# A fused attention and two-layer kernel: the second layer's weights are converted in the first layer's middle blocks and kept in DRAM

## The chip, the cores and the metric

The program runs on one core of one Trainium2 chip. The metric is the device time of one execution in microseconds (us), the median of the runs.

## What is computed

A recurrent linear attention over 4 batches, 8 heads, 768 steps and head size 48, then two feed-forward layers on the 3072 tokens (384 wide, 2048 hidden). The first has an ELU, the second h * cos(h). The weights of both layers arrive as float64.

```python
for t in range(S):
    cur = np.einsum('bhd,bhe->bhde', u[None] * kt, vt)
    y[:, :, t] = np.einsum('bhd,bhde->bhe', rt, state + cur)
    state = w[None, :, :, None] * state + np.einsum('bhd,bhe->bhde', kt, vt)
...
h = x @ w_in
g = np.where(h > 0.0, h, alpha * (np.exp(np.minimum(h, 0.0)) - 1.0))
x = (g @ w_out).astype(np.float32)
...
h = x @ w_in
g = h * np.cos(h)
return (g @ w_out).astype(np.float32)
```

## The kernel before

**Tiling.** Tokens go in 6 chunks of 512 (128 steps of 4 batches). A layer's 2048 hidden columns go in 16 tiles of 128 (`NF = 16`). The main loop runs over t from 0 to 193; one pass is called a slot here. `layer, block, f = t // 96, t // 16, t % 16`: a block is one layer on one chunk, 16 slots. Blocks 0 to 5 (slots 0 to 95) are the first layer, blocks 6 to 11 (slots 96 to 191) the second. In slot t TensorE does the 9 matmuls of 512 columns of `ffn_in` for tile f (line 300), the nonlinearity follows on ScalarE and VectorE, `split_g` cuts its result g into a rounded high part gh (ScalarE, line 307) and the rest gl (line 308), and two slots later TensorE does the 9 (first layer) or 12 (second) matmuls of `ffn_out_t` or `ffn_out` (lines 355, 364). Every product is made of three matmuls of high and low parts.

**Attention.** The attention of chunks 1 to 5 is laid into the slots of blocks 0 to 4, from chunk 2 on one unit (a batch pair and a head pair) for every two slots: an even slot has the Gram matmuls (line 194) and the masked copy of their result by VectorE (`copy_predicated`, line 199), an odd one the matmuls with values and state (lines 213, 217, 244) with the copy yu on ScalarE (line 227) and the state update st on VectorE (line 236). GpSimd prepares later units (lines 156, 157, 164, 181). A unit is loaded six slots ahead of its Gram matmuls and prepared four slots ahead. Block 5 has no attention. At a block's last slot `split_x` cuts the next chunk's x into xh (ScalarE, line 288, 3 operations) and xl (VectorE, line 289, 3 operations); the next block's first matmuls need them.

**Weights.** A weight tile (768 columns of float64 on 128 partitions, 768 KB) is loaded into wraw (`load_w`) and goes through seven operations of 768 elements: Abs (ScalarE, line 83), two `tensor_scalar` (VectorE, lines 89 and 92, `conv_low`), two `scalar_tensor_tensor` (VectorE, lines 99 and 102, `conv_high`), the rounded high part (ScalarE, line 111) and the low part by subtraction (GpSimd, line 112). The parts lie in wh and wl, and TensorE reads them. The first layer's 16 tiles are converted ahead of block 0 and in it. The second layer's are converted from block 5 on, into the same buffers, each behind the first layer's last use of it: in block 5 about one tile per slot (`convert(steps2)`), the last ones in block 6 at one step per slot. In blocks 0 and 5 gl is made by GpSimd (`busy`), elsewhere by VectorE.

**Order.** The whole order is written by hand: each engine runs its instructions in the order in which the program issues them, and waits at the first whose inputs or buffers are not there. All DMAs are issued by SyncE (SP), in one order.

Of the kernel before, what the change touches and what calls it, by code (L numbers as in the profile page):

```python
# [20 lines left out]
P = 128  # L21
# [18 lines left out]
def fused_kernel(ctx: ExitStack, tc: tile.TileContext, rk, nat, wcol, urow, r, k, v, wu, w1, w2, out):  # L40
# [9 lines left out]
    x2d = [dram.tile([P, KC, TB], F32, name=f"x2d{c}") for c in range(NC)]  # L50

    # ---------------------------------------------------------------- tables
# [24 lines left out]
    # A weight comes as a float64: words (low, high). Its magnitude's high word, read as a float32,  # L77
    # is monotone, so clamping that clamps the weight to float32's range.
# [18 lines left out]
    def conv_high(layer, f):  # L97
        t, x = wc_st[layer, f]
        nc.vector.scalar_tensor_tensor(  # L99
            out=x, in0=t[:, :, 1], scalar=-(1 << 30), in1=x, op0=ALU.bitwise_and, op1=ALU.bitwise_or  # L100
        )
        nc.vector.scalar_tensor_tensor(  # L102
            out=x, in0=t[:, :, 0], scalar=29, in1=x, op0=ALU.logical_shift_right, op1=ALU.bitwise_or
        )

    def conv_split(layer, f, eng):
        x = wc_st.pop((layer, f))[1]
        x = x.bitcast(F32)
        hi = wpool.tile([P, 2 * DM], F32R, tag=f"wh{f}", name=f"wh{f}")
        lo = wpool.tile([P, 2 * DM], F32R, tag=f"wl{f}", name=f"wl{f}")  # L110
        nc.scalar.activation(out=hi, in_=x, func=AF.Copy)  # L111
        eng.tensor_tensor(out=lo, in0=x, in1=hi.bitcast(F32), op=ALU.subtract)  # L112
        wt[layer, f] = (hi, lo)

    def conv_steps(layer):
        """Steps that turn a layer's weights into their two parts, three tiles at a time in turn."""

        def high(f):
            conv_high(layer, f)
            if f + 3 < NF:  # L120
                w_loads.append((layer, f + 3))

        steps = []
        for n in range(NF + 2):
            for f, step, fn in (
                (n - 2, "split", lambda f: conv_split(layer, f, nc.gpsimd)),
                (n - 1, "low", lambda f: conv_low(layer, f)),
                (n - 1, "high", high),
                (n, "abs", lambda f: conv_abs(layer, f)),
            ):  # L130
                if 0 <= f < NF:
                    steps.append((step, lambda fn=fn, f=f: fn(f)))
        return steps

    # ------------------------------------------------------------- attention
# [4 lines left out]
    def a_load(c, hb, j):  # L140
        if c == 0:
            # the first chunk lies where the last weight tiles will
            n = NF - 2 * HP + hb * HP + ORDER.index(j)
            trk = wpool.tile([RP, 2, 2, C], F32, tag=f"wl{n}", name="trk")
            tnat = wpool.tile([P, 3, 2, 2, D], F32, tag=f"wh{n}", name="tnat")
# [116 lines left out]
    def a_pack(c, hb, j):  # L262
        """Rows of a finished pair of heads into x: 96 of a k-tile, or the last 32 of each."""
# [9 lines left out]
        else:  # L273
            # the first chunk's last pair goes by itself: the first layer waits for it
# [9 lines left out]
    # ---------------------------------------------------------- feed-forward  # L284
# [40 lines left out]
    # cos(h) = sin(h + pi/2), the turn nearest to it taken off in two parts  # L325
# [43 lines left out]
    # ---------------------------------------------------------- general path  # L369
    def general():  # L370
        """Any decay: the recurrence step by step, then both layers in float32."""
# [40 lines left out]
        for layer in range(2):  # L412
            for f in range(NF):
# [4 lines left out]
                w = wpool.tile([P, 2 * DM], F32, tag=f"w{'hl'[layer]}{f}", name="wf")  # L418
# [61 lines left out]
    def tables():  # L480
        """pw[:, :, i] = w ** (i - 64), w128 = w ** 128, wn[s, h, d] = w ** (64 + s)"""
# [29 lines left out]
    def count_safe():  # L511
        """safe = 1 where every decay's powers over a chunk lie in range"""
# [14 lines left out]
    with tc.manual_schedule():  # L527
# [33 lines left out]
        steps, steps2 = conv_steps(0), conv_steps(1)  # L561
        put_off = []

        def convert(queue, n=None, hold=False):
            """The next n steps or those up to a tile's first, which is put off to the end of the slot."""
# [17 lines left out]
        # the first chunk's attention, its stages a unit apart  # L583
# [56 lines left out]
        for t in range(NT + 2):  # L640
            layer, block, f = t // L, t // NF, t % NF
            busy = layer == 0 and block in (0, NC - 1)
            if t < NT:
                ph = ffn_in(layer, f, xs[block], "G" if layer and f % 2 else "h")
            if layer == 0 or t == L:
# [4 lines left out]
                if t == 2 * NF:  # L650
                    count_safe()
                elif block == NC - 1:
                    if f == 0:
                        load_w(1, 0)
                        load_w(1, 1)
                        load_w(1, 2)
                    if f > 0:
                        convert(steps2)
# [16 lines left out]
            if layer == 0:  # L675
                end_slot()
            n = block + 1
# [12 lines left out]
            turning = t > L + 1  # L690
# [6 lines left out]
            (ffn_out if layer else ffn_out_t)(layer, f, *gs.pop(t - 2), acc)  # L697
            if f == NF - 1 and layer == 0:
# [11 lines left out]
            if turning:  # L710
                convert(steps2, 1)
                end_slot()
# [63 lines left out]
```

## Time and profile before

| | before |
|---|---|
| median of 3 runs | 1006.22 us (1004.83 to 1008.23) |
| span of the profiled execution | 1009.6 us |
| TensorE matmuls, busy | 946.1 us (94%) |
| VectorE busy | 700.6 us (69%) |
| ScalarE busy | 462.5 us (46%) |
| GpSimd busy | 272.5 us (27%) |
| moved by DMA | 70.35 MB |

The profile is of one execution, a run of its own; its span is the time from its first to its last instruction and lies 3.4 us above the median of the runs. Busy is the time in which an engine had an instruction under way. Matmuls overlap in the records, so a busy TensorE does not say how fast it runs; the time between the starts of two slots does.

### The profile page before, as it was taken

To read this page: it belongs to the slowest core of one execution; us is meant where nothing else is said; L and a number is where in the kernel's file an instruction comes from. 1 tells how busy PE (TensorE), PEld (TensorE's weight loads), DVE (VectorE), ACT (ScalarE), POOL (GpSimd) and SP (SyncE) were. 2 spreads that over 40 slices of the span, in tenths; PEclk is the share of its full clock that TensorE was granted. 3 is DMA by queue.
4 is the path that set the end of the run, shared out by engine and by line. 5 is a ranking of instruction groups with operands and counts; after the bars stand their busy time and mean duration, and the time that the engine had idled before them with its cause. 6 is when DMAs were issued, how large, how long until landed. Compare 5 with 4: busy or idle time off the path is not lost.

```text
span 1009.6 us, 13386 instructions
## 1 busy us (share of the span) xinstructions
PE 946.1 (94%) x5018; PEld 780.5 (77%) x5018; DVE 700.6 (69%) x1096; ACT 462.5 (46%) x770; POOL 272.5 (27%) x258
## 2 busy tenths in 40 slices
PE   6498889999999999999997779999999999999997
PEld 5366657777777777777775558899999999999996
DVE  6799974445544544534379999977877777777775
ACT  2454535334433433443465565544444445444443
POOL 6898973322322322211046541000000000000000
PEclk7599889999999999999999899999999999999999
DMA  9654620302322131130234321010010010100001
GB/s 251 197 166 148 195 74 28 108 23 73 89 68 75 54 91 44 42 91 3 106 108 165 114 84 63 1 63 1 1 63 1 1 63 1 63 1 1 32 1 35
DMA packets 28793, 70.35 MB, mean 70 GB/s; under 512 B 3760, under 2 KB 11568, under 8 KB 28720
## 3 DMA queue, kind: packets, MB, share of 16 engines
q1 hardware_dynamic: 28720, 69.42, 21.6%
q8 instruction: 41, 0.67, 0.3%
q14 instruction: 32, 0.26, 0.1%
HBM read 55.25 MB, written 9.44 MB: 64 GB/s over the span
## 4 chain that ended last, share of the span: by engine, by line
PE 72%; DVE 16%; issue 5%; POOL 2%; DMA 2%; ACT 2%; SPq 0%; DVEq 0%; ACTq 0%; POOLq 0%
PE ph L300 32%; PE acc L364 18%; PE acc L355 15%; DVE wx L99 4%; PE ys L217 3%; PE G L194 2%; PE ys L213 2%; DVE wx L92 2%; DVE g L320 1%; DVE wx L89 1%; DMA xraw<-yu 1%; DVE xl L289 1%; DVE wx L102 1%; DVE gl L308 1%; DVE trk L170 1%
## 5 line engine op out<-in xcount | busy, mean ns | idle before, releaser
L300 PE MATMUL ph<-xh,wh 128*128 128x512 f32 x576 | 229.5, 398 | 17.7 <-DVE g L320 17.7
L300 PE MATMUL ph<-xl,wh 128*128 128x512 f32 x576 | 228.8, 397 | 2.1 <-DVE xl L289 2.0
L300 PE MATMUL ph<-xh,wl 128*128 128x512 f32 x576 | 226.8, 394 | 0.0
L307 ACT ACTIVATE gh<-g 128x512 fp32r<-128x512 f32 x192 | 120.6, 628 | 191.6 <-DVE g L320 130.8
L308 DVE TENSOR_TENSOR gl<-g,gh 128x512 fp32r<-128x512 f32 x161 | 116.5, 724 | 68.6 <-ACT gh L307 68.5
L300 PEld LDWEIGHTS ph<-xh,wh 128*128 128x128 f32 x576 | 108.8, 189 | 42.9 <-DVE g L320 20.1
L364 PE MATMUL acc<-wh,gl 128*128 128x384 f32 x384 | 129.1, 336 | 3.7 <-DVE gl L308 3.7
L300 PEld LDWEIGHTS ph<-xl,wh 128*128 128x128 f32 x576 | 109.2, 190 | 28.4 <-DVE xl L289 3.5
L364 PE MATMUL acc<-wl,gh 128*128 128x384 f32 x384 | 129.4, 337 | 0.0
L364 PE MATMUL acc<-wh,gh 128*128 128x384 f32 x384 | 129.0, 336 | 0.0
L345 ACT ACTIVATE r<-r,halfpi 128x512 f32<-128x512 f32 x96 | 69.7, 726 | 125.0 <-DVE r L339 125.0
L300 PEld LDWEIGHTS ph<-xh,wl 128*128 128x128 f32 x576 | 109.1, 189 | 19.9
L355 PE MATMUL acc<-gh,wh 128*128 128x512 f32 x288 | 123.9, 430 | 0.4 <-ACT gh L307 0.4
L355 PE MATMUL acc<-gl,wh 128*128 128x512 f32 x288 | 114.8, 399 | 0.3 <-DVE gl L308 0.2
L355 PE MATMUL acc<-gh,wl 128*128 128x512 f32 x288 | 114.4, 397 | 0.0
L181 POOL TENSOR_SCALAR_AFFINE_SELECT A<-a 128x512 f32<-128x512 f32 x48 | 47.2, 983 | 241.4 <-DVE a L177 239.2
L333 DVE SCALAR_TENSOR_TENSOR r<-kk,ph 128x512 f32<-128x512 int32 x96 | 65.8, 686 | 56.3 <-ACT kk L328 56.2
L313 ACT ACTIVATE n<-ph 128x512 f32<-128x512 f32 x96 | 56.9, 593 | 94.9 <-PE ph L300 94.8
L328 ACT ACTIVATE kk<-ph 128x512 int32<-128x512 f32 x96 | 57.7, 601 | 73.9 <-PE ph L300 73.8
L112 POOL TENSOR_TENSOR wl<-wx,wh 128x768 fp32r<-128x768 f32 x32 | 74.1, 2317 | 45.6 <-ACT wh L111 30.4
L320 DVE SCALAR_TENSOR_TENSOR g<-e,ph 128x512 f32<-128x512 f32 x96 | 65.4, 681 | 27.8 <-ACT e L315 27.4
L347 DVE TENSOR_TENSOR g<-r,ph 128x512 f32<-128x512 f32 x96 | 65.8, 685 | 19.2 <-ACT r L345 19.2
(73 smaller groups left out, 1373.6 us busy)
## 6 DMA issues: line engine op xcount, KB each, us to landing
wraw<-in_w SPq DMA_DIRECT2D x32, 768.0 KB, 4.4
tnat<-in_nat SPq DMA_DIRECT2D x48, 288.0 KB, 4.4
trk<-in_rk SPq DMA_DIRECT2D x48, 224.0 KB, 4.3
x2d<-osb SPq DMA_DIRECT2D x6, 768.0 KB, 4.2
xraw<-x2d SPq DMA_DIRECT2D x6, 768.0 KB, 5.2
out_y<-yo SPq DMA_DIRECT2D x12, 384.0 KB, 3.1
xraw<-yu SPq DMA_DIRECT2D x22, 144.0 KB, 2.8
xraw<-yu SPq DMA_DIRECT2D x24, 32.0 KB, 1.9
```

Source lines behind the costliest of these rows:

```text
L112: eng.tensor_tensor(out=lo, in0=x, in1=hi.bitcast(F32), op=ALU.subtract)
L300: nc.tensor.matmul(ph, w[:, cs], z, start=(n == 0), stop=(n == 3 * KC - 1))
L307: nc.scalar.activation(out=gh, in_=g, func=AF.Copy)
L308: eng.tensor_tensor(out=gl, in0=g, in1=gh.bitcast(F32), op=ALU.subtract)
L313: nc.scalar.activation(out=n, in_=ph, func=AF.Relu, scale=-1.0)
L320: nc.vector.scalar_tensor_tensor(out=g, in0=e, scalar=-1.0, in1=ph, op0=ALU.add, op1=ALU.max)
L328: nc.scalar.activation(out=kk, in_=ph, func=AF.Copy, scale=1.0 / TWO_PI, bias=0.25)
L333: nc.vector.scalar_tensor_tensor(out=r, in0=kk, scalar=-C1, in1=ph, op0=ALU.mult, op1=ALU.add)
L345: nc.scalar.activation(out=r, in_=r, func=AF.Sin, bias=halfpi)
L347: nc.vector.tensor_tensor(out=g, in0=r, in1=ph, op=ALU.mult)
L355: nc.tensor.matmul(acc[m], w[:, cs], g, start=(f == 0 and n == 0), stop=(f == NF - 1 and n == 2))
L364: nc.tensor.matmul(acc[m][:, 0:DM], g[:, ts], w[:, DM:2 * DM], start=(f == 0 and n == 0), stop=(f == NF - 1 and n == 2),)
```

## The change

The second layer's 16 weight tiles are converted in slots 16 to 79, a tile in four slots. `second_weights` adds one part at the end of each slot: part 0 the two `tensor_scalar`, part 1 the first `scalar_tensor_tensor` (`conv_top`), part 2 the second (`conv_rest`), part 3 the high part on ScalarE, the low part on VectorE (it was on GpSimd) and the Abs of the next tile. Both parts are written over the raw tile, and the tile (768 KB) is stored to DRAM (`w2d`) in the part 0 that follows; the load of the tile after next waits for that store, since it takes the same buffer. In block 5 `fetch_weight(f)` reads tile f back into the first layer's buffer behind the last `ffn_out_t` that uses it, 14 slots ahead of its first use. wh and wl become halves of one tile. Nothing is converted in blocks 5 and 6 any more, and in block 5 gl is made by VectorE.

```diff
+    w2d = [dram.tile([P, 4 * DM], F32, name=f"w2d{f}") for f in range(NF)]
...
-        hi = wpool.tile([P, 2 * DM], F32R, tag=f"wh{f}", name=f"wh{f}")
-        lo = wpool.tile([P, 2 * DM], F32R, tag=f"wl{f}", name=f"wl{f}")
+    def split_w(x, parts, eng):
+        hi, lo = parts[:, 0:2 * DM], parts[:, 2 * DM:]
         nc.scalar.activation(out=hi, in_=x, func=AF.Copy)
         eng.tensor_tensor(out=lo, in0=x, in1=hi.bitcast(F32), op=ALU.subtract)
...
+    def second_weights(slot):
+        f, part = slot // 4, slot % 4
+        if slot == 0:
+            load_w(1, 0)
+            load_w(1, 1)
+            conv_abs(1, 0)
+        if part == 0:
+            if f > 0:
+                nc.sync.dma_start(out=w2d[f - 1], in_=split_tiles.pop(f - 1).bitcast(F32))
+            if f < NF:
+                conv_low(1, f)
+        elif part == 1:
+            if f + 2 < NF:
+                load_w(1, f + 2)
+            conv_top(1, f)
+        elif part == 2:
+            conv_rest(1, f)
+        else:
+            t, x = wc_st.pop((1, f))
+            parts = t.rearrange("p n l -> p (n l)").bitcast(F32R)
+            split_w(x.bitcast(F32), parts, nc.vector)
+            split_tiles[f] = parts
+            if f + 1 < NF:
+                conv_abs(1, f + 1)
+
+    def fetch_weight(f):
+        w = new_weight(f)
+        nc.sync.dma_start(out=w.bitcast(F32), in_=w2d[f])
+        wt[1, f] = (w[:, 0:2 * DM], w[:, 2 * DM:])
...
-            busy = layer == 0 and block in (0, NC - 1)
+            busy = layer == 0 and block == 0
...
-                elif block == NC - 1:
-                    if f == 0:
-                        load_w(1, 0)
-                        load_w(1, 1)
-                        load_w(1, 2)
-                    if f > 0:
-                        convert(steps2)
...
             if layer == 0:
                 end_slot()
+                if NF <= t <= 5 * NF:
+                    second_weights(t - NF)
...
             (ffn_out if layer else ffn_out_t)(layer, f, *gs.pop(t - 2), acc)
+            if layer == 0 and c == NC - 1:
+                fetch_weight(f)
...
-            if turning:
-                convert(steps2, 1)
-                end_slot()
```

VectorE at the end of block 1, from the last operations of slot 30 over slot 31 to the first of slot 32, before (g is the ELU, gl the rest of g, xl the rest of the next chunk's x):

```order
L170 TENSOR_TENSOR trk<-trk,pw 112x512
L320 SCALAR_TENSOR_TENSOR g<-e,ph 128x512
L308 TENSOR_TENSOR gl<-g,gh 128x512
L236 SCALAR_TENSOR_TENSOR st<-st,pows,ys 48x2x48 x2
L320 SCALAR_TENSOR_TENSOR g<-e,ph 128x512
L289 TENSOR_TENSOR xl<-xraw,xh 128x512 x3
L308 TENSOR_TENSOR gl<-g,gh 128x512
```

and now (wx is a weight tile under conversion, wraw the raw tile):

```order
L219 TENSOR_TENSOR trk<-trk,pw 112x512
L369 SCALAR_TENSOR_TENSOR g<-e,ph 128x512
L106 SCALAR_TENSOR_TENSOR wx<-wraw,wx 128x768
L357 TENSOR_TENSOR gl<-g,gh 128x512
L285 SCALAR_TENSOR_TENSOR st<-st,pows,ys 48x2x48 x2
L369 SCALAR_TENSOR_TENSOR g<-e,ph 128x512
L117 TENSOR_TENSOR wraw<-wx,wraw 128x768
L338 TENSOR_TENSOR xl<-xraw,xh 128x512 x3
L357 TENSOR_TENSOR gl<-g,gh 128x512
```

One operation of the conversion stands behind the ELU of each slot; in slot 31 the subtraction stands between the ELU and the three xl.

ScalarE over slot 31, the same place, before (n and e belong to the ELU):

```order
L313 ACTIVATE n<-ph 128x512
L315 ACTIVATE e<-n 128x512
L227 ACTIVATE yu<-ys 112x256
L288 ACTIVATE xh<-xraw 128x512 x3
L307 ACTIVATE gh<-g 128x512
```

and now:

```order
L362 ACTIVATE n<-ph 128x512
L364 ACTIVATE e<-n 128x512
L276 ACTIVATE yu<-ys 112x256
L116 ACTIVATE wraw<-wx 128x768
L84 ACTIVATE wx<-wraw 128x768
L337 ACTIVATE xh<-xraw 128x512 x3
L356 ACTIVATE gh<-g 128x512
```

The high part of one tile and the Abs of the next stand between yu and the three xh.

SP in block 1 from slot 22 to slot 26, before (trk and tnat are a unit's loads, xraw<-yu the packing of attention results into x):

```order
L269 DMA xraw<-yu 32x256
L270 DMA xraw<-yu 16x256
L271 DMA xraw<-yu 16x256
L272 DMA xraw<-yu 32x256
L149 DMA trk<-in_rk 112x512
L150 DMA tnat<-in_nat 128x576
L149 DMA trk<-in_rk 112x512
L150 DMA tnat<-in_nat 128x576
L149 DMA trk<-in_rk 112x512
L150 DMA tnat<-in_nat 128x576
```

and now:

```order
L318 DMA xraw<-yu 32x256
L319 DMA xraw<-yu 16x256
L320 DMA xraw<-yu 16x256
L321 DMA xraw<-yu 32x256
L198 DMA trk<-in_rk 112x512
L199 DMA tnat<-in_nat 128x576
L198 DMA trk<-in_rk 112x512
L199 DMA tnat<-in_nat 128x576
L160 DMA w2d_77<-wraw 128x1536
L75 DMA wraw<-in_w 128x1536
L198 DMA trk<-in_rk 112x512
L199 DMA tnat<-in_nat 128x576
```

The store of a tile and the load into its buffer stand between the loads of two units.

## Rows read from the trace of the kernel before

**Rows 1.** Busy time by stretch: blocks 2, 5, 6 and 7; clock, DMA last.

```profile
248.90:335.89 86.99, 86.79 (x516) 67.21 (x514) 42.51 (x88) 36.10 (x62) 24.13 (x32) 1.00 0.22 67
502.47:592.07 89.60, 74.13 (x289) 56.51 (x288) 82.65 (x75) 50.54 (x79) 50.41 (x27) 0.94 0.35 124
592.07:663.90 71.83, 68.31 (x331) 59.40 (x331) 64.60 (x93) 39.90 (x63) 9.97 (x5) 1.00 0.09 34
663.90:730.57 66.67, 66.67 (x338) 60.49 (x338) 51.86 (x86) 31.93 (x53) 0.00 (x0) 1.00 0.07 24
```

**Rows 2.** Timeline, TensorE in block 4 behind its attention: first matmuls of two slots.

```profile
490.11 0.39 PE L300 MATMUL ph<-xh,wh 128*128 128x512 f32 x1
...
494.23 0.39 PE L300 MATMUL ph<-xh,wh 128*128 128x512 f32 x1
```

**Rows 3.** Waits: us, times, longest; block 5, then block 6.

```profile
PE ph L300 <- DVE g L320: 13.0, 10, 1.8
...
PE acc L364 <- DVE gl L308: 2.9, 4, 1.1
```

**Rows 4.** Timeline, operations of the conversion at different places.

```profile
80.66 1.24 DVE L99 SCALAR_TENSOR_TENSOR wx<-wraw,wx 128x768 int32<-128x768 int32 x1
...
525.36 2.51 DVE L102 SCALAR_TENSOR_TENSOR wx<-wraw,wx 128x768 int32<-128x768 int32 x1
...
607.01 0.83 ACT L111 ACTIVATE wh<-wx 128x768 fp32r<-128x768 f32 x1
...
613.40 0.55 DVE L89 TENSOR_SCALAR wx<-wx 128x768 f32<-128x768 f32 x1
613.99 0.56 DVE L92 TENSOR_SCALAR wx<-wx 128x768 int32<-128x768 int32 x1
...
617.77 0.95 DVE L99 SCALAR_TENSOR_TENSOR wx<-wraw,wx 128x768 int32<-128x768 int32 x1
...
620.89 0.90 ACT L83 ACTIVATE wx<-wraw 128x768 f32<-128x768 f32 x1
```

**Rows 5.** Timeline of block 2, VectorE and ScalarE in slots 45 and 46.

```profile
320.17 0.82 DVE L308 TENSOR_TENSOR gl<-g,gh 128x512 fp32r<-128x512 f32 x1 [0.76 <-ACT gh L307]
...
323.42 0.64 DVE L236 SCALAR_TENSOR_TENSOR st<-st,pows,ys 48x96 f32<-48x96 f32 x2 [2.43 <-ACT yu L227]
...
324.08 0.69 DVE L320 SCALAR_TENSOR_TENSOR g<-e,ph 128x512 f32<-128x512 f32 x1
...
325.26 0.63 ACT L307 ACTIVATE gh<-g 128x512 fp32r<-128x512 f32 x1 [1.88 <-PE acc L355]
...
325.93 0.69 DVE L308 TENSOR_TENSOR gl<-g,gh 128x512 fp32r<-128x512 f32 x1 [1.16 <-ACT gh L307]
...
328.04 0.78 DVE L199 COPY_PREDICATED A<-mask,G 128x256 f32<-128x256 uint32 x2 [1.41 <-PE G L194]
```

**Rows 6.** Timeline, end of slot 31 and slot 32.

```profile
247.12 1.66 ACT L288 ACTIVATE xh<-xraw 128x512 fp32r<-128x512 f32 x3
...
248.52 1.89 DVE L289 TENSOR_TENSOR xl<-xraw,xh 128x512 fp32r<-128x512 f32 x3
...
248.90 0.39 PE L300 MATMUL ph<-xh,wh 128*128 128x512 f32 x1
...
249.37 0.39 PE L300 MATMUL ph<-xl,wh 128*128 128x512 f32 x1
...
251.34 0.19 PE L518 MATMUL okp<-ok,ones 112*1 112x4 f32 x2 [0.20 <-DVE ok L514]
```

**Rows 7.** Page, DMA issues: KB each, median us to landing.

```profile
x2d<-osb SPq DMA_DIRECT2D x6, 768.0 KB, 4.2
xraw<-x2d SPq DMA_DIRECT2D x6, 768.0 KB, 5.2
```

**Rows 8.** Timeline, a unit's load on SP, and its first use on GpSimd.

```profile
315.15 0.40 SPq L149 DMA_DIRECT2D trk<-in_rk  x1
...
341.52 0.60 POOL L156 TENSOR_TENSOR tnat<-tnat 128x192 f32<-128x192 f32 x1
```

More of the change, by code (lines that the diff above doesn't have):

```diff
@@ L95, in conv_low, with conv_top @@
         )
-    def conv_high(layer, f):
+    def conv_top(layer, f):
         t, x = wc_st[layer, f]
@@ L101, in conv_high, with conv_rest @@
         )
+    def conv_rest(layer, f):
+        t, x = wc_st[layer, f]
         nc.vector.scalar_tensor_tensor(
@@ L104, in conv_high, with new_weight, conv_split @@
         )
-    def conv_split(layer, f, eng):
-        x = wc_st.pop((layer, f))[1]
-        x = x.bitcast(F32)
-        hi = wpool.tile([P, 2 * DM], F32R, tag=f"wh{f}", name=f"wh{f}")
-        lo = wpool.tile([P, 2 * DM], F32R, tag=f"wl{f}", name=f"wl{f}")
+    def conv_high(layer, f):
+        conv_top(layer, f)
+        conv_rest(layer, f)
+    def split_w(x, parts, eng):
+        hi, lo = parts[:, 0:2 * DM], parts[:, 2 * DM:]
         nc.scalar.activation(out=hi, in_=x, func=AF.Copy)
         eng.tensor_tensor(out=lo, in0=x, in1=hi.bitcast(F32), op=ALU.subtract)
-        wt[layer, f] = (hi, lo)
+    def new_weight(f):
+        return wpool.tile([P, 4 * DM], F32R, tag=f"w{f}", name=f"w{f}")
+    def conv_split(layer, f):
+        x = wc_st.pop((layer, f))[1]
+        w = new_weight(f)
+        split_w(x.bitcast(F32), w, nc.gpsimd)
+        wt[layer, f] = (w[:, 0:2 * DM], w[:, 2 * DM:])
     def conv_steps(layer):
@@ L125, in conv_steps @@
             for f, step, fn in (
-                (n - 2, "split", lambda f: conv_split(layer, f, nc.gpsimd)),
+                (n - 2, "split", lambda f: conv_split(layer, f)),
                 (n - 1, "low", lambda f: conv_low(layer, f)),
@@ L133, in conv_steps @@
         return steps
+    split_tiles = {}
+    def second_weights(slot):
[23 more added lines that the diff above has]
+    def fetch_weight(f):
+        w = new_weight(f)
+        nc.sync.dma_start(out=w.bitcast(F32), in_=w2d[f])
+        wt[1, f] = (w[:, 0:2 * DM], w[:, 2 * DM:])
     units = {}
@@ L143, in a_load @@
             n = NF - 2 * HP + hb * HP + ORDER.index(j)
-            trk = wpool.tile([RP, 2, 2, C], F32, tag=f"wl{n}", name="trk")
-            tnat = wpool.tile([P, 3, 2, 2, D], F32, tag=f"wh{n}", name="tnat")
+            both = wpool.tile([P, 4 * DM], F32, tag=f"w{n}", name="both")
+            m = 4 * C
+            trk = both[0:RP, 0:m].rearrange("p (x b t) -> p x b t", x=2, b=2)
+            tnat = both[:, m:m + 12 * D].rearrange("p (x e b d) -> p x e b d", x=3, e=2, b=2)
         else:
@@ L411, in general @@
         ws = {}
-        for layer in range(2):
-            for f in range(NF):
+        for f in range(NF):
+            both = wpool.tile([P, 4 * DM], F32, tag=f"w{f}", name="wf")
+            for layer in range(2):
                 load_w(layer, f)
@@ L417, in general @@
                 conv_high(layer, f)
-                w = wpool.tile([P, 2 * DM], F32, tag=f"w{'hl'[layer]}{f}", name="wf")
+                w = both[:, layer * 2 * DM:(layer + 1) * 2 * DM]
                 nc.scalar.activation(out=w, in_=wc_st.pop((layer, f))[1].bitcast(F32), func=AF.Copy)
@@ L560, in fused_kernel @@
                 items.setdefault((c - 1) * NF + it, []).append(fn)
-        steps, steps2 = conv_steps(0), conv_steps(1)
+        steps = conv_steps(0)
         put_off = []
@@ L689, in fused_kernel @@
                 continue
-            turning = t > L + 1
             layer, c, f = (t - 2) // L, (t - 2) // NF % NC, (t - 2) % NF
```

## The prediction

> **What bounds the kernel now.** I read the busy time by stretch first, a block at a time [rows 1]. In blocks 2 and 7 TensorE's busy time is the whole stretch (66.67 of 66.67 us) and VectorE has room (42.51 of 86.99): these blocks go at TensorE's pace. Blocks 5 and 6 don't: TensorE is busy in 74.13 of 89.60 us and in 68.31 of 71.83. In block 5 VectorE is busy in 82.65 of the 89.60 us, so VectorE sets the pace there; its granted clock column also falls to 0.94, a mix of TensorE's two levels, while every other block in the group shows 1.00.
>
> The waits say what TensorE waits for [rows 3]. In block 5 it waits 13.0 us in 10 pieces of up to 1.8 us for the ELU result, which stands on VectorE behind a tile's conversion; in block 6 it waits 2.9 us for gl at the conversion's steps. The timeline shows what a first-layer slot costs when nothing but the feed-forward is left in it: the slots behind block 4's last attention follow each other at 490.11 and 494.23, that is 4.12 us [rows 2].
>
> One operation of the conversion has several prices [rows 4]. The same `scalar_tensor_tensor` takes 0.95 us in the second layer, 1.24 us in block 0 beside GpSimd's small products, and 2.51 us in block 5 beside GpSimd's subtraction of a whole tile. The two `tensor_scalar` take 0.55 and 0.56, the Abs 0.90, the high part 0.83.
>
> **What the change removes.** Block 5 loses every conversion, so its 16 slots can go at the 4.12 us of [rows 2]: those slots have already what block 5 gets, gl on VectorE and no attention. 16 x 4.12 = 65.9, against 89.60: 23.7 us gained. VectorE then has an ELU and a gl per slot, 0.69 + 0.69 [rows 5], a third of the slot. Block 6 becomes like block 7: 71.83 - 66.67 = 5.2 us gained [rows 1]. The layer's switch lies in block 6 too; nothing of it but the conversion is slow for a reason that I can see, so I take all of it.
>
> **What it adds in blocks 1 to 4.** VectorE gets per tile 0.55 + 0.56, two operations of 0.95 to 1.24, and the subtraction, which no row shows on VectorE; as an operation with two inputs of 768 elements I take 0.95, its like in [rows 4], with 2.51 as the upper end. That is 4.0 to 4.6 us per four slots, about 1.1 us a slot. I ask what stands behind each piece. In an odd slot it comes after the ELU, which starts at 324.08 and takes 0.69; the next instruction, gl, waited 1.16 us for gh, and the one after it, the masked copy, waited 1.41 us for the Gram matmuls [rows 5]. Together that is 2.57 us of cover for a piece of about 0.95. In an even slot gl waited 0.76 and the state update after it 2.43 us: 3.19 us for a piece of 1.1 to 1.24. Delaying gl itself costs nothing, since TensorE uses it a slot later. So the pieces are hidden, and hidden even at 2.51 us each, barely.
>
> On ScalarE the high part and the Abs (0.83 + 0.90 = 1.73) stand every fourth slot, an odd one, between yu and gh, and gh waited 1.88 us there for its buffer [rows 5]. Hidden, with 0.15 left. On VectorE the subtraction waits for the high part, which ends about when the ELU ends.
>
> On SP a tile's store waits for the subtraction, and the next load of a raw tile waits until that store has landed; what stands behind it is a later unit's trk and tnat. A store of this size lands in 4.2 us [rows 7]. In the trace such a load was issued at 315.15, and GpSimd first used it at 341.52 [rows 8]. With the store issued at about the same time, the load would go out some 4.2 us later and still be over 20 us early. Hidden. SP runs ahead of the slots in this way, so the first two raw tiles, whose buffers are free by then, land before their Abs in slot 16.
>
> In block 5 each read-back is issued 14 slots before its use. At the 5.2 us of the same size [rows 7], one behind the other, the last lands 16 x 5.2 = 83 us after the first was issued at the end of slot 82. Its use is in slot 111, 28 slots of 4.12 to 4.17 us (66.67 / 16), some 116 us, after that. Hidden.
>
> **The step that is not hidden** is the last slot of blocks 1 to 4, where the order puts the last part ahead of the next chunk's x. Before, the three xh start at 247.12 and the three xl at 248.52, and TensorE's first two kinds of matmul of block 2 start at 248.90 and 249.37, right behind them [rows 6]. Now ScalarE does 1.73 us first: the first xh (1.66 / 3 = 0.55) ends at 247.12 + 1.73 + 0.55 = 249.4, and TensorE starts 0.5 us late. VectorE puts the subtraction ahead: xl starts at 248.52 + 0.95 = 249.5, the first is ready at 250.1, 0.75 us late, the last at 251.4. In slot 32 a small matmul (okp) also waits for VectorE, which is now about 1.1 us late. I take 1.1 us for each of the four, since the others lack okp but the fourth lacks the attention matmuls that would cover a part: 4.4 us. The bounds are 0, if x is read early enough by another path, and 1.73 + 0.95 = 2.7 each, 10.7 in all, if both engines' additions add up.
>
> **Sum.** 1009.6 - 23.7 - 5.2 + 4.4 = 985.1 us for the span, a gain of 24.5. The profiled execution is 3.4 us above the median of the runs; I take the same gain off the median: 1006.2 - 24.5 = 981.7 us. From no change at the seams (-28.9) to the full seams (-18.2) that is 977.3 to 988.0.
>
> **Rivals.** (1) The pieces don't fit: VectorE and GpSimd hold each other up. For it: the same instruction took 0.95, 1.24 and 2.51 us according to what GpSimd did at the time [rows 4]. Against: in block 2 GpSimd has only small operations (24.13 us in 86.99). It decides when an odd slot's piece passes 2.57 us; at 2.51 with a gl drawn out from 0.69 to 0.82 [rows 5] a pair of slots would lose some 0.2 to 0.3, times 32 pairs 6 to 10 us: 988 to 992. The Trainium skill speaks for it: SBUF — State Buffer, Who interferes with whom, says that VectorE with two SBUF inputs and GpSimd reading SBUF take a shared port in turn, for a whole instruction each. By that rule's worst a piece of 0.95 us waits for three of GpSimd's products of 0.60 us each [rows 8] and takes 2.75 us, which an even slot's cover of 3.19 still holds, so the sum by the rule is the same and only this rival's chance hangs on it. The 1.24 us of block 0 agrees with a short wait; no row shows the middle blocks.
> (2) The seams cost nothing: 977.3. For it, only that TensorE starts a block some tenths behind xl; against, the order above.
> (3) The read-back becomes the bound: the tiles come late in block 6. The last one is late from 116 / 16 = 7.2 us per transfer; at 8.7 us it is 16 x 8.7 - 116 = 23 us late, and nearly all of the gain is gone: 1005. Against: 5.2 in [rows 7].
> (4) Slower than before: the stores hold SP. The next raw tile's load waits for a store, the units' loads stand behind it, and GpSimd's preparation and the Gram matmuls of blocks 1 to 4 wait for those. Once a store takes longer to land than a tile's four slots, 86.99 / 4 = 21.7 us [rows 1], SP sets the pace, and each of the 16 tiles adds what it is over; the gain is used up at 21.7 + 24.5 / 16 = 23.2 us, and at 24 us the time is 981.7 + 16 x 2.3 = 1018. Against: 4.2 us for the same size going the same way [rows 7]. The Trainium skill, DMA: Bandwidth & Descriptors, Anatomy of one DMA — SWDGE (gpsimd) path, says of transfers that another queue issues that the receipt of the write is most of their fixed cost, heaviest where the target is HBM. Here a store isn't slower than a read-back of the same size (4.2 against 5.2 us).
> That the change doesn't do what it says I exclude: the order shows blocks 5 and 6 free of conversions.
>
> **Chances.** The forecast 0.74, rival 1 0.11, rival 2 0.07, a mixture short of the gain (block 5 somewhat above 4.12 a slot) 0.04, rival 3 0.02, rival 4 0.02. What a measurement of this kernel can tell from no change is about 0.3%, 3 us, by the scatter of the three runs. All but rivals 3 and 4 are faster: 0.96. The range takes in the seams' bounds and rival 1: 976 to 991.
>
> **What would show it.** Right: slots of block 5 at 4.12 us, block 6 at 66.7, blocks 2 and 3 at 86 to 88 with the excess in their first slot only, VectorE some 17 us busier per block there, no wait of TensorE for a Gram operand or for a weight tile. Wrong: pairs of slots in blocks 1 to 4 above 86.99 / 8 = 10.9 us, a longer `scalar_tensor_tensor` there than 1.3 us, waits of GpSimd for tnat, or of TensorE for a w tile in block 6.

## The result and the profile after

The changed kernel takes 985.04 us (median of 4 runs, 983.3 to 986.56), the kernel before 1006.21 (1004.83 to 1008.23). The ratio is 0.9773, with a 95% interval of 0.9748 to 0.9799: faster by 20 to 25 us. The forecast was 981.7 us with a range of 976 to 991, that is a ratio of 0.9757. The profiled execution's span went from 1009.6 to 984.6 us, 25.0 less (forecast 24.5).

The page's first part has each engine's busy time in the new kernel:

```profile
PE 939.1 (95%) x5018; PEld 778.6 (79%) x5018; DVE 695.5 (71%) x1128; ACT 463.0 (47%) x770; POOL 237.2 (24%) x226
```

VectorE is busy about as long as before (700.6 us, now 695.5) with 32 operations more (1096, now 1128), and TensorE too; GpSimd has lost the subtractions and block 5's gl (272.5 us, now 237.2). What differs is the place of the work, and the windows of blocks 2, 5, 6 and 7, which answer to [rows 1], show where (us, then busy time of PE, PEld, DVE, ACT and POOL, granted clock, DMA share, GB/s):

```profile
248.94:336.78 87.84, 87.33 (x514) 67.12 (x514) 59.70 (x108) 42.08 (x71) 31.07 (x32) 1.00 0.42 138
505.36:572.02 66.66, 66.32 (x288) 54.11 (x289) 25.89 (x39) 33.58 (x56) 0.00 (x0) 1.00 0.54 190
572.02:638.59 66.57, 66.57 (x332) 59.68 (x330) 49.36 (x81) 33.13 (x54) 0.00 (x0) 1.00 0.19 60
638.59:705.25 66.66, 66.66 (x337) 60.47 (x337) 51.90 (x86) 31.93 (x53) 0.00 (x0) 1.00 0.07 25
```

Block 5 fell from 89.60 to 66.66 us, and VectorE in it from 82.65 to 25.89. Block 6 fell from 71.83 to 66.57 and is now as long as block 7. Block 2 carries 17.2 us more on VectorE and is only 0.85 us longer. The granted clock is 1.00 in all of them; block 5 had 0.94.

The timeline of TensorE in block 5, the first matmuls of two slots, as in [rows 2]:

```profile
522.59 0.62 PE L349 MATMUL ph<-xh,w 128*128 128x512 f32 x2
...
526.71 0.62 PE L349 MATMUL ph<-xh,w 128*128 128x512 f32 x2
```

They are 4.12 us apart. All that TensorE waits for from block 1 to block 6 stands in three rows of the waits (us in all, times, longest), where [rows 3] had 13.0 us in block 5 and 2.9 in block 6:

```profile
PE ph L349 <- ACT xh L337: 1.3, 4, 0.5
PE ph L349 <- DVE xl L338: 0.3, 1, 0.3
PE okp L568 <- DVE ok L564: 0.2, 1, 0.2
```

Nothing there waits for an ELU, a Gram operand or a weight tile; what is left are the block ends. The page's DMA issues (KB each, median us to landing) have the two new transfers beside those of [rows 7]:

```profile
w2d<-wraw SPq DMA_DIRECT2D x16, 768.0 KB, 3.6
w<-w2d SPq DMA_DIRECT2D x16, 768.0 KB, 4.2
```

How the pieces lie in the middle blocks shows in VectorE's timeline over slots of block 2, from the subtraction of one tile to the second `scalar_tensor_tensor` of the next:

```profile
292.08 0.69 DVE L369 SCALAR_TENSOR_TENSOR g<-e,ph 128x512 f32<-128x512 f32 x1
292.69 0.95 DVE L117 TENSOR_TENSOR wraw<-wx,wraw 128x768 fp32r<-128x768 f32 x1
293.93 0.69 DVE L357 TENSOR_TENSOR gl<-g,gh 128x512 fp32r<-128x512 f32 x1 [0.29 <-ACT gh L356]
296.04 0.78 DVE L248 COPY_PREDICATED A<-mask,G 128x256 f32<-128x256 uint32 x2 [1.41 <-PE G L243]
...
298.17 0.56 DVE L90 TENSOR_SCALAR wx<-wx 128x768 f32<-128x768 f32 x1
298.76 0.84 DVE L93 TENSOR_SCALAR wx<-wx 128x768 int32<-128x768 int32 x1
299.52 1.08 DVE L357 TENSOR_TENSOR gl<-g,gh 128x512 fp32r<-128x512 f32 x1
302.25 0.64 DVE L285 SCALAR_TENSOR_TENSOR st<-st,pows,ys 48x96 f32<-48x96 f32 x2 [1.64 <-ACT yu L276]
...
303.51 0.95 DVE L100 SCALAR_TENSOR_TENSOR wx<-wraw,wx 128x768 int32<-128x768 int32 x1
```

In the odd slot the piece of 0.95 took the place of the wait for gh: gl waited 1.16 us there in [rows 5] and waits 0.29 now. The masked copy waits 1.41 us for the Gram matmuls, exactly as before. In the even slot gl's wait of 0.76 is gone and the state update's fell from 2.43 to 1.64. The pieces fill waits.

In an even slot they also meet GpSimd's preparation of a unit, here on both engines:

```profile
308.94 1.46 POOL L213 TENSOR_TENSOR tnat<-tnat,wn 128x192 f32<-128x192 f32 x1
308.99 0.95 DVE L106 SCALAR_TENSOR_TENSOR wx<-wraw,wx 128x768 int32<-128x768 int32 x1
309.86 1.09 DVE L357 TENSOR_TENSOR gl<-g,gh 128x512 fp32r<-128x512 f32 x1
```

VectorE's piece keeps its 0.95 us, but GpSimd's product, which took 0.60 before, is drawn out to 1.46, and the gl behind it to 1.09 ([rows 5] had 0.69 and 0.82). The second `tensor_scalar` takes 0.84 (0.56 alone). In block 2 GpSimd's same 32 operations take 31.07 us in place of 24.13. So the two engines do hold each other up there; it falls into waits, and TensorE does not wait for it.

The whole difference by blocks, from the starts of the slots: 22.9 us are gained in block 5 and 5.3 in block 6; blocks 1 to 4 together took 340.2 before and take 343.5 now, 3.3 lost; that is 24.9 gained. The rest is within 0.5.

### The profile page after: what moved, and what is told of

It reads as the page before. It is cut to its first block, busy times and chain, and to the rows that moved or that the text cites. A ratio compares the mean times of both kernels' runs of the same rounds, so it can differ in the third digit from the quotient of the medians.

```text
span 984.6 us, 13424 instructions
## 1 busy us (share of the span) xinstructions
PE 939.1 (95%) x5018; PEld 778.6 (79%) x5018; DVE 695.5 (71%) x1128; ACT 463.0 (47%) x770; POOL 237.2 (24%) x226
## 4 chain that ended last, share of the span: by engine, by line
PE 83%; DVE 8%; DMA 4%; issue 2%; ACT 1%; SPq 0%; DVEq 0%; ACTq 0%
PE ph L349 37%; PE acc L413 20%; PE acc L404 18%; PE ys L266 3%; PE ys L262 2%; PE G L243 2%; DVE wx L100 2%; DMA both<-in_rk 1%; DMA xraw<-yu 1%; DVE wx L93 1%; DMA both<-in_nat 1%; DVE wx L90 1%; DVE trk L219 1%; DVE g L369 1%; DVE xl L338 1%
## 5 line engine op out<-in xcount | busy, mean ns | idle before, releaser
L349 PE MATMUL ph<-xh,w 128*128 128x512 f32 x1152 | 361.1, 395 | 3.7 <-DVE g L369 2.3
L349 PEld LDWEIGHTS ph<-xh,w 128*128 128x128 f32 x1152 | 215.6, 189 | 45.9 <-ACT xh L337 3.1
L349 PE MATMUL ph<-xl,w 128*128 128x512 f32 x576 | 228.0, 396 | 2.5 <-DVE xl L338 2.4
L404 PE MATMUL acc<-gh,w 128*128 128x512 f32 x576 | 205.9, 412 | 0.0
L413 PE MATMUL acc<-w,gh 128*128 128x384 f32 x768 | 196.2, 336 | 0.0
L413 PEld LDWEIGHTS acc<-w,gh 128*128 128x128 f32 x768 | 140.1, 188 | 8.0
L404 PEld LDWEIGHTS acc<-gh,w 128*128 128x128 f32 x576 | 109.9, 191 | 29.7 <-issue 1.9
L349 PEld LDWEIGHTS ph<-xl,w 128*128 128x128 f32 x576 | 108.9, 189 | 29.8 <-DVE xl L338 4.9
L413 PE MATMUL acc<-w,gl 128*128 128x384 f32 x384 | 128.6, 335 | 0.8 <-DVE gl L357 0.8
L404 PE MATMUL acc<-gl,w 128*128 128x512 f32 x288 | 114.2, 397 | 0.0
```

The lines of the kernel that those rows point to most:

```text
L349: nc.tensor.matmul(ph, w[:, cs], z, start=(n == 0), stop=(n == 3 * KC - 1))
L404: nc.tensor.matmul(acc[m], w[:, cs], g, start=(f == 0 and n == 0), stop=(f == NF - 1 and n == 2))
L413: nc.tensor.matmul(acc[m][:, 0:DM], g[:, ts], w[:, DM:2 * DM], start=(f == 0 and n == 0), stop=(f == NF - 1 and n == 2),)
```

## The experiments

Each kernel differs from one of the two by the edit shown; two of them build on an earlier one, as said there. Spans are of one profiled execution, and where no median is given the kernel ran once. Whole spans differ between executions (last section), so kernels that ran once are read by the lengths of blocks 1 to 6; blocks 1 to 4 agree within 0.05 us between executions of kernels that do the same there.

### What the block ends cost: x cut first

```diff
             if layer == 0:
                 end_slot()
+                if f == NF - 1 and block + 1 < NC:
+                    xs[block + 1] = [split_x(xin[block + 1], k, x_tags) for k in range(KC)]
                 if NF <= t <= 5 * NF:
                     second_weights(t - NF)
...
-            if n < NC:
-                if f == NF - 1:
-                    xs[n] = [split_x(xin[n], k, x_tags) for k in range(KC)]
-            elif n < 2 * NC:
+            if NC <= n < 2 * NC:
```

> The changed kernel with one edit: in the last slot of a block the next chunk's x is cut into xh and xl ahead of the second layer's conversion part, not behind it. My theory: the four block ends of blocks 1 to 4 cost 3.6 us in the changed kernel only because the high part and the Abs (ScalarE) and the subtraction (VectorE) stand ahead of xh and xl. Then the first two slots of a block together are back at before's lengths (the pair behind block 1 at 11.22 us, now 12.10), and the span falls by 3 to 4 us from 984.6, to some 981. Rival: the seams are longer for another reason (the packed x lands later behind the stores on SP); then xh starts when it does now, and the span stays within 0.5 us.

In the changed kernel the end of block 1 looks like this (timeline, the rows that answer to [rows 6]):

```profile
246.73 0.84 ACT L116 ACTIVATE wraw<-wx 128x768 fp32r<-128x768 f32 x1
247.46 0.90 ACT L84 ACTIVATE wx<-wraw 128x768 f32<-128x768 f32 x1
248.12 0.95 DVE L117 TENSOR_TENSOR wraw<-wx,wraw 128x768 fp32r<-128x768 f32 x1
248.24 1.68 ACT L337 ACTIVATE xh<-xraw 128x512 fp32r<-128x512 f32 x3
248.94 0.73 PE L349 MATMUL ph<-xh,w 128*128 128x512 f32 x2 [0.27 <-ACT xh L337]
248.99 1.89 DVE L338 TENSOR_TENSOR xl<-xraw,xh 128x512 fp32r<-128x512 f32 x3
```

xh stands behind the high part and the Abs, xl behind the subtraction, as forecast. Counted over the last slot of a block and the first of the next, the four seams are 0.88, 0.88, 0.82 and 1.01 us longer than before, 3.6 in all.

With x cut first the windows of blocks 1 and 2 are:

```profile
157.53:244.15 86.62, 86.62 (x514) 67.14 (x513) 58.31 (x103) 41.58 (x70) 31.13 (x32) 1.00 0.38 122
244.15:332.00 87.85, 86.79 (x516) 67.22 (x514) 59.71 (x108) 42.07 (x71) 31.08 (x32) 1.00 0.42 138
...
```

Block 1 is at the length of the kernel before to a hundredth, and so are blocks 3 and 4 (86.26 and 80.32). Block 2 isn't, with 87.85 us against 86.99 before [rows 1]: its first slot, slot 32, takes 6.24 us (5.38 before), and in the waits stands

```profile
PE okp L568 <- DVE ok L564: 1.1, 1, 1.1
```

where the small product of the count of safe decays now waits behind the subtraction. The slots up to the first of block 5 are together 2.7 us shorter than in the changed kernel, a little under the expected 3 to 4: the seams are what the theory says, except in slot 32. The median is 979.36 us, the ratio 0.9716 (0.9697 to 0.9734). The profiled execution was the slowest of six (985.04), so the expected 981 can't be read from its span of 983.0. The ratio is 0.0057 below that of the changed kernel, some 5.7 us, more than the slots give; where the rest comes from stays open.

### The last seam: the count moved to block 5

```diff
-                if t == 2 * NF:
+                if t == 5 * NF + 4:
                     count_safe()
...
-        okp = psum.tile([1, HP], F32, tag="h", name="okp", bufs=2)
+        okp = psum.tile([1, HP], F32, tag="ys", name="okp")
```

> The kernel with x cut ahead of the conversion part at a block's end, and besides the count of safe decays (ok, okp) not in slot 32 but in slot 84, in block 5, with its small product in a PSUM buffer that the attention no longer uses. In the earlier run with x cut first, slot 32 stayed at 6.24 us (5.38 in the kernel before), because okp waited 1.06 us for ok on VectorE, behind the subtraction. My theory: in slot 32 that was all that was left, so the slot goes to 4.98 us like the same slot of the other blocks, 1.3 us less; block 5 loses nothing, since VectorE is idle for two thirds of each slot there. A span 1.3 us under that of the earlier run at the same pace of TensorE, and a ratio to before of 0.970 (the earlier run's 0.9716 less 1.3 / 1008). Rival: the wait only moves to slot 84 or to the next slot's masked copy; then 0.

x is cut first here too, by the edit above. Windows of blocks 1, 2 and 5:

```profile
157.38:243.98 86.60, 86.60 (x513) 67.12 (x512) 58.34 (x103) 41.61 (x70) 31.14 (x32) 1.00 0.37 122
243.98:330.58 86.60, 86.60 (x513) 67.14 (x512) 59.19 (x104) 42.12 (x71) 31.07 (x32) 1.00 0.42 140
...
497.16:563.86 66.70, 66.63 (x292) 54.10 (x292) 26.99 (x44) 34.30 (x57) 0.00 (x0) 1.00 0.54 190
```

TensorE is busy all of blocks 1 and 2, slot 32 takes 5.00 us, and slot 84 takes 4.46 in place of 4.12, so 0.3 of the 1.3 was lost again, in part as the rival said. Blocks 1 to 5 together are 3.7 us shorter than in the changed kernel. The median is 976.57 us, the ratio 0.9699 (0.9679 to 0.9719), near the expected 0.970. Its interval lies below that of the change (0.9748 to 0.9799), so this kernel is faster than the changed one too. It overlaps that of x cut first (0.9697 to 0.9734): the gain of 1.0 us over that kernel rests on the slots alone.

### How much the middle slots cover: one piece four and eight times

```diff
-        nc.vector.scalar_tensor_tensor(
-            out=x, in0=t[:, :, 1], scalar=-(1 << 30), in1=x, op0=ALU.bitwise_and, op1=ALU.bitwise_or
-        )
+        for _ in range(4 if layer else 1):
+            nc.vector.scalar_tensor_tensor(
+                out=x, in0=t[:, :, 1], scalar=-(1 << 30), in1=x, op0=ALU.bitwise_and, op1=ALU.bitwise_or
+            )
```

> The changed kernel with the first scalar_tensor_tensor of a second-layer tile issued four times in place (it ORs the same bits each time, so that the result is the same): VectorE's piece in one odd slot of every four is 3.8 us, not 0.95. Theory A (the prediction's rival 1: an odd slot covers 2.57 us and what is over is lost at once): 16 times 3.8 - 2.57 = 1.23 us, some 20 us, a span of about 1004. Theory B (the cover is larger, since the masked copy of the Gram matrix that comes late has itself slack until the next odd slot's matmuls read it): no change, a span within 1.5 us of 984.6, and no new wait of TensorE in blocks 1 to 4.

Blocks 1 to 4 took 87.05, 87.85, 87.14 and 81.43 us, the changed kernel's lengths within 0.01; the span was 983.0. VectorE's timeline around one such piece:

```profile
282.32 3.93 DVE L101 SCALAR_TENSOR_TENSOR wx<-wraw,wx 128x768 int32<-128x768 int32 x4
...
286.17 0.69 DVE L358 TENSOR_TENSOR gl<-g,gh 128x512 fp32r<-128x512 f32 x1
286.77 0.77 DVE L249 COPY_PREDICATED A<-mask,G 128x256 f32<-128x256 uint32 x2
```

gl and the copy no longer wait for anything, both come late, and TensorE waits no longer than in the changed kernel. Theory A is refuted: it would have cost 20 us. Over blocks 1 to 4 VectorE's waits for the Gram matmuls, gh and yu fell from 37.8 + 16.6 + 41.5 to 18.6 + 5.7 + 29.6 us: 42 of the 48 us that the 48 more operations take.

The same with 8 in place of 4:

> The changed kernel with the first scalar_tensor_tensor of a tile issued eight times (7.6 us of VectorE in one odd slot of every four; the result is the same). Issued four times, 3.8 us, it cost nothing. If the cover is 2.57 us of one odd slot alone, it would cost 80 us; that is already refuted. Theory: the cover of a run of four slots is what VectorE's waits leave in them, since gl, the masked copy and the state update each have a slot of slack: VectorE was busy 59 to 60 of 87.5 us per block, that is about 6.9 us idle in four slots; 6.65 us more than once just about fill it, so a part is lost where the masked copy A comes too late for the matmuls with values of the next odd slot: 1 to 2 us per tile, 15 to 30 us in all, a span of about 1000 to 1015, with TensorE waiting for A or gl.

The span was 1009.9 us, and blocks 1 to 4 took 94.78, 95.60, 93.91 and 87.25. Behind each of the first three pieces of blocks 1 to 3 the next odd slot is 1.50 us longer (7.34 for 5.84), and now TensorE waits for the copy; the waits from block 1 on:

```profile
PE ys L267 <- DVE A L249: 12.1, 11, 1.1
PE ph L350 <- ACT xh L338: 7.7, 4, 2.2
```

Eight operations, twice the 3.93 us of four, cost 1.50, so a piece in an odd slot is covered up to 7.9 - 1.5 = 6.4 us, where the prediction had 2.57. In block 4 the loss is 0.39 us and the cover 7.5. The rest of the loss is at the block ends, where xh waits for what is behind the long piece.

### The conversion undivided

```diff
-            if f < NF:
-                conv_low(1, f)
         elif part == 1:
             if f + 2 < NF:
                 load_w(1, f + 2)
+            conv_low(1, f)
             conv_top(1, f)
-        elif part == 2:
             conv_rest(1, f)
-        else:
             t, x = wc_st.pop((1, f))
...
             split_tiles[f] = parts
+        elif part == 3:
             if f + 1 < NF:
                 conv_abs(1, f + 1)
```

> The changed kernel with a tile's conversion not in four pieces: the two tensor_scalar, the two scalar_tensor_tensor, the high part and the subtraction all stand at the end of part 1, one odd slot of four, and part 3 has only the Abs of the next tile. VectorE's piece there is 0.55 + 0.56 + 2 x 0.95 + 0.84 = 3.85 us and a wait for ScalarE's 0.83 us, some 4.7 us in all. Theory A (cover of 2.57 us): 16 x 2.1 = 34 us longer, about 1018: the piecewise order is what makes the change pay. Theory B (slack behind the masked copy): within 3 us of 984.6, so the place of the conversion matters and its division into four does not.

Blocks 1 to 4 took 88.00, 88.73, 87.99 and 81.32 us, 2.6 more than in the changed kernel (span 985.1): theory B. The loss is in one slot per block, the third (6.35 us for 4.98; 5.23 in block 4), 4.4 us in all, and the seams give 1.8 back. The timeline there shows why:

```profile
262.85 0.84 ACT L116 ACTIVATE wraw<-wx 128x768 fp32r<-128x768 f32 x1 [4.46 <-DVE wx L106]
263.60 1.55 ACT L745 ACTIVATE osb<-acc 128x512 f32<-128x512 f32 x3
...
264.23 0.50 PE L402 MATMUL acc<-gh,w 128*128 128x512 f32 x1 [1.30 <-ACT osb L745]
```

ScalarE stands at the high part for 4.46 us, behind it the copy of a finished chunk out of PSUM, and TensorE waits 1.30 us for that PSUM buffer. So the division into pieces is worth 2.6 us here, net of what the seams give back, and through ScalarE's queue; 4.7 us of VectorE work at one place are hidden in every other odd slot, as the cover of 6.4 us says.

### What made block 5 slow: company or work

The kernel before, with the second layer's subtraction and block 5's gl on VectorE:

```diff
-                (n - 2, "split", lambda f: conv_split(layer, f, nc.gpsimd)),
+                (n - 2, "split", lambda f: conv_split(layer, f, nc.vector if layer else nc.gpsimd)),
...
-            busy = layer == 0 and block in (0, NC - 1)
+            busy = layer == 0 and block == 0
```

> The kernel before with one edit: in blocks 5 and 6 the second layer's subtraction and block 5's gl are made by VectorE, so that GpSimd has nothing to do there. The conversion stays in blocks 5 and 6. Theory A (block 5 was slow because VectorE and GpSimd held each other up: 2.51 us for an operation that takes 0.95 alone): VectorE's work per slot is 0.55 + 0.56 + 2 x 0.95 + 0.84 for a tile and 0.69 + 0.69 for ELU and gl, 5.2 to 5.4 us; block 5 goes from 89.6 to about 83 to 86 us, block 6 gains some 2: the kernel is 5 to 9 us faster, and the operation takes 0.95 in block 5. Theory B (block 5 was slow by the amount of work on VectorE, the long durations being its own): the two added operations of 0.84 and 0.69 us lengthen each slot by some 1.5 us, and the kernel is about 20 us slower.

The ratio is 0.9939 (0.9920 to 0.9959), 6 us faster; block 5 took 88.49 us, block 6 69.35. The groups of VectorE's instructions from 515 to 580 us, in block 5 (count, busy us, mean ns, idle before):

```profile
L99 DVE SCALAR_TENSOR_TENSOR wx<-wraw,wx 128x768 int32<-128x768 int32 x11 | 10.6, 959 | 0.4
L112 DVE TENSOR_TENSOR wl<-wx,wh 128x768 fp32r<-128x768 f32 x11 | 10.5, 959 | 0.5
...
L308 DVE TENSOR_TENSOR gl<-g,gh 128x512 fp32r<-128x512 f32 x11 | 7.6, 692 | 7.1 <-ACT gh L307 7.1
```

In the profiles the two blocks give 3.6 us; slot 16 began 2.7 us earlier, in a stretch that the edit doesn't touch. Why the medians of 10 and 15 runs differ by more than 3.6 us stays open. The mechanism of theory A is there: with GpSimd idle the operation takes 0.96 us, not 2.51. But block 5 gained 1.1 us, not 4 to 7. A slot there takes 6.10 us (6.18 before): 0.55 + 0.56 + 3 x 0.96 + 0.68 + 0.69 = 5.36 of work (the subtraction at 0.96, where the expectation had 0.84), and 0.76 in which gl waits for gh. In the kernel before, the same slot was 0.55 + 0.56 + 1.94 + 2.51 + 0.67 = 6.23 us, each of the two `scalar_tensor_tensor` behind an operation of GpSimd (the 2.51 of [rows 4] behind the subtraction, the first behind gl):

```profile
523.09 1.41 POOL L308 TENSOR_TENSOR gl<-g,gh 128x512 fp32r<-128x512 f32 x1 [2.22 <-ACT gh L307]
523.38 1.94 DVE L99 SCALAR_TENSOR_TENSOR wx<-wraw,wx 128x768 int32<-128x768 int32 x1
```

At 0.96 each they would have made it 3.70, under 4.12. So by this sum GpSimd's company made VectorE's slot too long there, and in this kernel GpSimd's work, moved over, does. No kernel here takes the company away without giving VectorE the work; of the kernels that ran, those that convert nothing in block 5 reach the 4.12.

The same question for block 0, put to the best kernel with gl on VectorE there too:

```diff
-            busy = layer == 0 and block == 0
+            busy = False
```

> As the kernel with x cut first and the count in block 5, and besides gl on VectorE, not GpSimd, in block 0 too, where the first layer's own conversion runs (111 to 113 us for slots 1 to 16, both engines busy for some 100 of 115 us, gl 1.75 us each on GpSimd). Theory A (the two engines hold each other up in block 0, as they did in block 5): VectorE gets 16 x 0.69 = 11 us more work, but its 26 conversion operations of 1.50 and 1.68 us come down towards 0.95, up to 17 us less: block 0 gets 0 to 6 us shorter. Theory B (work counts, not company): block 0 gets up to 11 us longer.

The median is 989.42 us, the ratio 0.9823 (0.9803 to 0.9843): 12 to 13 us slower than without this edit, all in block 0 (124.85 us for 111.65), even beyond theory B. In this block the two `scalar_tensor_tensor` did come down, from 1.50 and 1.67 to 1.05 and 1.04 us on average. But gl takes 11.4 us, waits another 11.4 for gh in 15 pieces, and one of the `tensor_scalar` got longer, from 0.96 to 1.87 on average. VectorE's and GpSimd's timeline at one tile:

```profile
112.08 2.08 POOL L117 TENSOR_TENSOR w<-wx,w 128x768 fp32r<-128x768 f32 x1 [3.61 <-ACT w L116]
112.50 2.08 DVE L93 TENSOR_SCALAR wx<-wx 128x768 int32<-128x768 int32 x1
```

An operation of 0.56 us that begins 0.42 us behind GpSimd's subtraction takes 2.08 and ends 0.42 us behind it, at 114.58. The Trainium skill, SBUF — State Buffer, Who interferes with whom, says that `tensor_scalar` can enter a mode that takes the port shared with GpSimd, and that whoever issues first has it for the whole instruction; the two rows agree.

### The transfers: stores and read-backs doubled

```diff
-                nc.sync.dma_start(out=w2d[f - 1], in_=split_tiles.pop(f - 1).bitcast(F32))
+                for _ in range(2):
+                    nc.sync.dma_start(out=w2d[f - 1], in_=split_tiles[f - 1].bitcast(F32))
+                split_tiles.pop(f - 1)
...
-        nc.sync.dma_start(out=w.bitcast(F32), in_=w2d[f])
+        for _ in range(2):
+            nc.sync.dma_start(out=w.bitcast(F32), in_=w2d[f])
```

> The changed kernel with each store to w2d and each read-back issued twice (same data, same place). For the stores (the prediction's rival 4): SP is held for at most twice 4.2 us of a tile's 21.9 us, so blocks 1 to 4 stay as they are, within 0.3 us each. For the read-backs (its rival 3): if the second waits on SP until the first has landed, the 16 tiles come one behind the other at 2 x 4.2 = 8.4 us, tile f is there 8.4 (f + 1) us after the first issue and is due 14 x 4.12 + 4.14 f us after it; from tile 12 on it is late, the last by some 15 us, and block 6 gets 15 us longer with TensorE waiting for the tile. If the two go side by side, nothing: block 6 stays at 66.6.

Blocks 1 to 4 took 87.05, 87.85, 87.13 and 81.43 us: SP is far from being held by the stores. Block 6 took 84.97, 18.4 more, near the expected 15, but not by the expected cause. The 32 read-backs went out from 515.77 to 617.26 us, 3.27 apart, so a pair took 6.55 and not 8.4 us, and by the formula of the expectation no tile is late. What was late stands in the timeline of SP, ScalarE and TensorE:

```profile
617.26 0.32 SPq L182 DMA_DIRECT2D w<-w2d  x1
617.63 0.42 SPq L751 DMA_DIRECT2D x2d<-osb  x1
624.25 0.32 SPq L676 DMA_DIRECT2D xraw<-x2d  x1
628.50 0.63 ACT L340 ACTIVATE xh<-xraw 128x512 fp32r<-128x512 f32 x1 [18.51 <-DMA xraw<-x2d]
...
631.17 1.01 PE L416 MATMUL acc<-w,gh 128*128 128x384 f32 x2 [14.06 <-ACT gh L359]
```

The store of the last first-layer chunk and the read of the second layer's next x stand behind the read-backs on SP. ScalarE waits 18.51 us for that x, and gh stands behind it. In the changed kernel the same read goes out at 587.54 and x is first used at 612.77: about 20 us of slack, at 5.2 us per read.

### GpSimd again: the subtraction, and block 5's gl

```diff
-            split_w(x.bitcast(F32), parts, nc.vector)
+            split_w(x.bitcast(F32), parts, nc.gpsimd)
```

> The changed kernel with the low part's subtraction in part 3 back on GpSimd, the rest as it is. Theory A (the prediction's rival 1: VectorE and GpSimd hold each other up wherever both are busy): the subtraction takes some 2 to 2.6 us on GpSimd, as in block 0, and the VectorE operations beside it (state update, xl, gl, the next tensor_scalar) come out longer by up to as much; but with a cover of about 6 us on VectorE nothing is lost in the middle slots, and the span stays within 1 us. At the block ends xl no longer stands behind the subtraction on VectorE, but xh still stands behind the high part and the Abs: the seams stay between half and all of 3.6 us. Theory B (the subtraction on VectorE was needed): GpSimd's preparation of units comes late by 2.5 us per tile, TensorE waits for A or the Gram operands, 10 us or more.

The middle slots stayed as they were, but the seams got longer, not shorter: blocks 1 to 5 together 412.2 us, 2.1 more than in the changed kernel (span 986.3). At the end of block 1 the timeline has

```profile
245.76 1.85 POOL L117 TENSOR_TENSOR wraw<-wx,wraw 128x768 fp32r<-128x768 f32 x1 [1.78 <-ACT wraw L116]
...
247.03 2.33 DVE L338 TENSOR_TENSOR xl<-xraw,xh 128x512 fp32r<-128x512 f32 x3 [0.71 <-ACT xh L337]
```

xl takes 2.33 us beside GpSimd's subtraction (1.89 without), and still waits for xh. The first three seams are 0.4 to 0.5 us longer than in the changed kernel, the last 0.9: there TensorE waits 1.22 us for xl, where it waited 0.34. Both theories missed this sign.

The other kernel makes block 5's gl on GpSimd, as before the change:

```diff
-            busy = layer == 0 and block == 0
+            busy = layer == 0 and block in (0, NC - 1)
```

> The changed kernel with gl in block 5 on GpSimd, as before the change. Theory A: block 5's gain is from the conversion's absence alone; gl on GpSimd takes 0.8 to 2 us, the result is used a slot of 4.12 us later, and block 5 stays at 66.7 us, the span within 0.5 us at the same pace of TensorE. Theory B: gl on VectorE is part of the gain; gl on GpSimd comes too late for the second matmul of a tile, and slots get longer than 4.2 us: block 5 some 70 us or more.

Block 5 took 66.68 us, with gl at 1.33 us on GpSimd (span 979.1): theory A. The engine of gl is no part of the gain.

## Why the prediction was right

**Block 5, -23.7 forecast.** The slots go at 4.12 us, as read from [rows 2]; 22.9 us were gained, since the block's first slot takes 4.87 us: 4.57 as before, which the sum overlooked, and 0.3 of the fourth seam. The engine of gl has no part in it (66.68 us with gl on GpSimd). GpSimd's company made the conversion's operations long there, but taking it away by moving GpSimd's work to VectorE gained only 1.1 us; taking the conversion out gained 22.9.

**Block 6, -5.2.** 5.3 us were gained; TensorE's wait for gl is gone.

**Seams, +4.4.** They cost 3.6 us, counted over the last slot of a block and the first of the next. The term was the right step with a size 0.8 too large, and x cut first with the count moved takes it back. At slot 31, measured from its start, xh comes 1.52 us later than before (forecast 1.73), and TensorE's first matmul of the next block 0.44 later (0.5). The xl start 0.87 later, and okp's wait is as long as it was, behind a VectorE 0.87 late: that makes the 0.88 where the prediction put 1.1. Half of it lies in the block's last slot; the text had all of it in the next block's first.

**Hidden pieces.** Right, and for more reason than given: the cover of 2.57 us in an odd slot counted only the waits up to the masked copy. The copy itself may come late, since TensorE reads it in the next odd slot; the two runs with longer pieces give 6.4 us. So rival 1 could not have decided at 2.57 us: its durations of up to 2.51 us would have been hidden. Its price was too high by its own terms, too: 2.51 + 0.82 - 0.69 - 2.57 is 0.07 us a pair, some 2 us in 32 pairs, not 6 to 10. Its mechanism is there in part. In the odd slots GpSimd was idle while the pieces ran, and in the even slots VectorE's `scalar_tensor_tensor` kept its 0.95 us (951 ns on average) while GpSimd was busy beside it, in 14 of 16 cases; GpSimd's product, the second `tensor_scalar` and gl were drawn out instead.

**The sum.** It came out 0.4 us off (24.9 for 24.5), in part by luck: without the fourth seam's 0.3 block 5 gave 0.5 us less than forecast, and the seams cost 0.8 us less.

**Transfers.** Stores land in 3.6 us and read-backs in 4.2, below the rows they were priced by. Rival 4 is far off. Rival 3 was priced at the wrong victim: the first thing that late read-backs hold up is not a tile but the second layer's x behind them on SP.

**The median.** It fell by 21.2 us, the profiled span by 25.0 and the forecast was 24.5 for both. The ratio's interval, 20 to 25 us, holds the forecast. Taking the span's gain off the median assumed that the profiled executions lie alike above their medians. They don't: a run's time is some 2 us above its span (1006.84 and 1005.1 in a later run of the kernel before), so that the profiled execution lay about 5 us above the median before and 1.5 us now (986.56 against 985.04). That is nearly all of the gap of 3.8; what made the one execution slow stays open.

## What to carry to other kernels

Work that fills one stage's engine can be free in another where that engine waits: look there not only for the wait behind the inserted piece, but for when the next thing is needed by the engine that sets the pace. Put such a piece behind what the next stage is waiting for; the order at four block ends was worth 2.7 us here, and a small product that waited there another 1. And before a transfer is called hidden, look at what stands behind it in its queue, not only at its own due time.

## What the runs showed that was not expected

An operation's length depends on the neighbour: 768 elements with two inputs take 0.95 or 0.96 us with GpSimd idle and up to 2.51 behind an operation of GpSimd, and GpSimd's product of 0.60 us takes up to 1.46 beside one of VectorE. But moving GpSimd's work to VectorE to spare them gained 1.1 us in block 5 and 2.5 in block 6, and lost 13 in block 0, where the moved operation takes 11.4 us and waits as long again, in order, for its own input.

TensorE's pace differs from one execution to the next at a granted clock of 1.00. The second block of the second layer, where TensorE is busy throughout, took 66.66 us in the profile of the changed kernel, and in two others (x cut first, then with the count moved):

```profile
633.58:700.99 67.41, 67.41 (x337) 61.08 (x337) 51.94 (x86) 31.88 (x53) 0.00 (x0) 1.00 0.07 24
```

```profile
630.14:696.49 66.35, 66.35 (x337) 60.37 (x337) 51.95 (x86) 31.94 (x53) 0.00 (x0) 1.00 0.07 25
```

Over the six blocks of that layer this is 6 us, more than the seams are worth. The start differs too: slot 0 begins at 48.96 us in the profile with one piece four times and at 45.81 with x cut first, though neither edit touches anything ahead of it. What sets either stays open. It is why small changes were read here from the lengths of the early blocks, and why a difference of medians is not put down to an edit beyond what its slots show.
